# A transformer block on one core: the last part of the program in another order, from the same list scheduler with other constants

## Chip, core and metric

The kernel runs on one core of one Trainium2 chip. Its time is device time in microseconds (us) of one launch, from the first to the last instruction of the program with what the device adds around them. Less is better. The engines of a core work beside each other, each strictly through its own queue of instructions: PE (TensorE, matmuls), PEld (its weight loads), DVE (VectorE), ACT (ScalarE), POOL (GpSimd) and SP (SyncE, which here only issues transfers). An instruction waits at the head of its queue until what it needs is there, and everything behind it waits too.

## The reference

One block with adaptive layer norm: windowed causal attention with 32 heads of 16, and a gated feed-forward layer. Cut to what is computed (S = 2048 rows, D = 512, F = 1792, window W = 256, float32 throughout):

```python
mod = (silu(c) @ w_mod).reshape(1, 6, 1, -1)
sa, ca, ga, sb, cb, gb = (mod[:, i] for i in range(6))
h = layernorm(x) * (1 + ca) + sa
q, k, v = heads(h @ wqkv)                      # 32 heads of 16
p = softmax(where(0 <= i - j < W, q @ k.T * 16 ** -0.5, -1e9))
x = x + ga * (merge(p @ v) @ wo)
h = layernorm(x) * (1 + cb) + sb
x = x + gb * ((silu(h @ w1) * (h @ w3)) @ w2)
```

## The kernel before

Float32 precision is had from pairs: a matrix is split in a high part (a rounded copy, made by ACT) and a low part (the rest, made by DVE or POOL with a subtraction), and a product of two matrices is three matmuls, high by high, high by low and low by high (`PARTS`). Every operand that PE multiplies in the later stages thus needs one ACT and one DVE or POOL instruction ahead of it.

**Start and attention.** The rows are four blocks b = 0 to 3 of 512 rows, the heads eight groups g of four. Attention is 32 units u = (g, b). Each unit makes scores (L750, with a mask added by PE at L753, or by DVE at L758, or with two blocks merged by DVE at L768), probabilities on ACT (L762, L771), window masks on POOL (`affine_select`, L778 and L795) and values (L726), and stores its output `os` to `o_dr[b]` in HBM (L818). Ahead of its scores run the maxima of its rows: trial scores (L500), DVE maxima (L507), their transposition (L522, L527), and a small transfer of them into `ring` (L531). The order of all of this was written out by hand as due times (`X`, `Y`).

**The end, from a list schedule.** Whatever falls due after `TS` = 232 of those time units (the last three units), and all that follows attention, is ordered by the class `Sched`: each operation has an engine, an estimated duration, a key (a wish for when) and dependencies, and `deal()` goes through model time, always giving the engine its ready operation with the smallest key. The remaining attention operations are put in at fixed model times, `us(t)`, which `TW` stretches. Transfers are modelled by one wire of `RATE` GB/s. PSUM banks are handed out by use, at most `CAPS` of each use at once. Keys and the choice of engine come from the table `K`. The model sets nothing but the order: on the chip each engine follows its queue and waits where data are missing.

What it orders, in the program's words:

- `load_wo` (L1040, splits at L962 and L963): the output projection's weights `wo`.
- `o_sums` (L1061, L1065, L1066): softmax sums are read from `o_dr`, inverted by DVE (`RECIPROCAL`), and stored to `r_dr`; once for head groups 0 to 5 (tile `wqr`) and once for the last two (tile `mT`).
- `o_part(b, k)` for four slices k of each block: load of the attention output (L1083), load of the inverted sums spread over rows (L1078), their product (L1095), high part (ACT, L1087), low part (L1090). The tile is called `o` for b = 0, 2, 3 and `x1b` for b = 1; the loads land in `qkr`/`qk` (k = 0, 1) and `wq` (k = 2, 3).
- `o_proj(b)`: for each of the block's four row tiles, four groups of three matmuls (L1107), one group for each k; then `add_stats` adds x (L978, DVE), and gathers mean and squares (L983, L986 on ACT). x comes by L1046 into `x1a` and `x1b`.
- `ln_rstd` (L997 DVE, L1000 POOL, L1003 DVE) and `ln2`: the normalised rows (L1228 on ACT), their transposition (L1242 on PE), scale and shift (L1246 on ACT), differences (L1259) and splits (L1265 ACT, L1267 DVE or POOL) into the operands `b`.
- The feed-forward layer in two halves of the rows, each as seven pairs p of column tiles. A half uses a seven-product scheme in place of eight: `up` makes seven products of six matmuls each (L1371) with operands called B11, T2, T3, T1, B21, T4, B22; sums on DVE (L1399, L1403) and POOL (L1415); SiLU on ACT (L1394); splits of the result (L1443, L1446). `down` (L1465) multiplies by `w2` and L1470 adds to x. Weights come by `load_w` (L1165) and `load_w2` (L1209), split at L962 and L963. `half_rows`, `half_sums` and `load_b` prepare the second half's seven operands through HBM (L1346), again split at L962 and L963.

The table's entries that matter below: `by` (engines of L1095 and L1090 for each b and k), `su` (engine of the weights' low parts), `be` (engine of the low part of each second-half operand), and keys such as `pe`, `pl` (when `o_part` is wanted), `xb` (when x1a and x1b are), `w0` (the first weights).

## Time and profile before

| | us |
|---|---|
| median of 3 runs | 983.88 (979.4 to 986.37) |
| the profiled execution | 981.63 |
| its span, first to last instruction | 979.6 |
| PE busy in it | 942.7 (96%) |
| DVE, ACT, POOL busy | 746.8, 555.6, 503.9 |
| mean granted clock of PE | 0.990 |

Of the span, attention takes the stretch up to about 484 us, the output projection and the second layer norm that up to about 540 us, the first half of the feed-forward layer that up to about 740 us, and the second half the rest. A busy matmul at a halved granted clock counts as busy, so PE loses time in two ways: idle, and busy at a low clock. Both have to be read stretch by stretch. In the views below, a row of the timeline has the start, the time that the (merged) instructions took, engine, line, operation, tile written and tiles read, and in brackets the idle time of the engine ahead of it and what ended it. A row of the windows has the stretch, then busy time of PE, PEld, DVE, ACT and POOL (with the number of instructions), the granted clock of PE, the mean busy share of the 16 DMA engines, and GB/s.

### The profile page before, as it was taken

Reading aid. Unit: us, or ns where it says so; the run is one execution under the profiler, and the core shown is the slowest. Engines: PE = TensorE matmul, PEld = TensorE weight load, DVE = VectorE, ACT = ScalarE, POOL = GpSimd, SP = SyncE. Lnnn points to the kernel's source line nnn. Section 1 sums busy time; section 2 is a strip of 40 time slices with the busy share of each in tenths; the row PEclk is TensorE's granted clock in tenths of the full one; section 3 lists DMA queues with packets and bytes.
Section 4 is the critical chain, followed back from the end, with each engine's and each line's share of the span. In section 5 each row is a group of like instructions: output and inputs, shape, how many; then the busy total and the mean of one; then the engine's idle time right before and its main releaser. Section 6 shows DMA issues by size and latency. Waiting matters only on the chain.

```text
span 979.6 us, 17120 instructions
## 1 busy us (share of the span) xinstructions
PE 942.7 (96%) x5316; PEld 718.4 (73%) x5316; DVE 746.8 (76%) x2049; ACT 555.6 (57%) x1252; POOL 503.9 (51%) x725
## 2 busy tenths in 40 slices
PE   5999999999999999998889999999999999999998
PEld 3578777677767776775567888888887888888886
DVE  7776799898989899898566685866769765576545
ACT  3333787887878787876568945233445443423330
POOL 7441787777767786864464754654416122111320
PEclk9999999999999999999899999999999999999999
DMA  8521354444444444435893576756434432212102
GB/s 288 184 87 34 117 180 150 142 153 143 158 158 142 142 143 143 142 121 177 225 264 89 177 254 217 243 173 202 151 124 145 152 119 77 79 48 88 44 22 86
DMA packets 80670, 141.63 MB, mean 145 GB/s; under 512 B 9538, under 2 KB 22338, under 8 KB 80580
## 3 DMA queue, kind: packets, MB, share of 16 engines
q1 hardware_dynamic: 79860, 139.50, 44.0%
q10 hardware_dynamic: 720, 1.05, 0.4%
q8 instruction: 42, 0.69, 0.3%
q14 instruction: 48, 0.39, 0.1%
HBM read 85.72 MB, written 34.61 MB: 123 GB/s over the span
## 4 chain that ended last, share of the span: by engine, by line
PE 78%; DVE 7%; POOL 5%; DMA 4%; ACT 2%; issue 2%; SPq 1%; POOLq 0%; DVEq 0%; ACTq 0%
PE mx L1371 12%; PE st L1371 11%; PE mx L500 7%; PE st L1465 7%; PE pj L447 7%; PE st L750 7%; PE po L726 6%; PE mx L1465 6%; PE pj L1371 5%; PE st L664 3%; PE pj L1465 2%; POOL pt L778 2%; POOL qk L465 2%; PE mx L1107 1%; DMA w<-w2g 1%
## 5 line engine op out<-in xcount | busy, mean ns | idle before, releaser
L507 DVE CUSTOM_DVE_ANT_0 junk<-mx,mskq 128x384 bf16<-128x384 f32 (+2 forms) x512 | 256.4, 527 | 28.2 <-PE mx L500 26.7
L750 PE MATMUL st<-ring 100*128 100x384 f32 (+2 forms) x512 | 156.3, 347 | 5.1 <-ACT pt L771 3.3
L500 PE MATMUL mx<-ring 96*128 96x384 f32 (+2 forms) x512 | 155.1, 341 | 4.4 <-DVE st L768 1.5
L778 POOL TENSOR_SCALAR_AFFINE_SELECT pt<-pt 128x256 f32<-128x256 f32 x268 | 108.3, 407 | 68.9 <-ACT pt L771 58.5
L447 PE MATMUL pj<-hT,wq 128*128 128x512 f32 x384 | 136.5, 405 | 1.5 <-DVE hT L364 1.2
L500 PEld LDWEIGHTS mx<-ring 96*128 96x128 f32 x512 | 93.9, 190 | 37.5 <-DVE mt L507 24.6
L771 ACT ACTIVATE pt<-st 128x256 f32<-128x256 f32 x268 | 96.1, 386 | 44.0 <-DVE st L768 36.4
L1415 POOL TENSOR_TENSOR t<-t,t 128x512 f32<-128x512 f32 x28 | 40.3, 1439 | 155.6 <-DVE t L1403 153.4
L750 PEld LDWEIGHTS st<-ring 100*128 100x128 f32 x512 | 95.9, 191 | 27.1 <-issue 8.6
L726 PE MATMUL po<-pt,vS 128*17 128x384 f32 (+2 forms) x1408 | 97.3, 393 | 3.6 <-POOL pt L778 3.2
L465 POOL TENSOR_TENSOR qk<-qkr,qk 128x512 fp32r<-128x512 f32 x64 | 82.7, 1292 | 15.9 <-ACT qkr L453 15.6
L768 DVE COPY_PREDICATED st<-later,st 128x128 f32<-128x128 uint8 x268 | 72.3, 292 | 11.4 <-PE st L750 8.2
L447 PEld LDWEIGHTS pj<-hT,wq 128*128 128x128 f32 x384 | 71.9, 191 | 8.6 <-DVE hT L364 1.5
L963 POOL TENSOR_TENSOR w<-w,w 128x512 fp32r<-128x512 f32 (+2 forms) x31 | 42.4, 1385 | 63.2 <-ACT w L962 63.2
L726 PEld LDWEIGHTS po<-pt,vS 128*17 128x17 f32 x1408 | 33.1, 98 | 49.8 <-issue 20.9
L762 ACT ACTIVATE pt<-st 128x384 f32<-128x384 f32 (+2 forms) x128 | 52.8, 434 | 18.7 <-DVE st L758 12.6
L1371 PE MATMUL st<-b,w 128*128 128x512 f32 x246 | 61.6, 392 | 0.1
L876 POOL TENSOR_TENSOR e<-e 128x128 f32<-128x128 f32 x64 | 41.9, 659 | 31.0 <-DMA e<-in_w 27.8
L1394 ACT ACTIVATE g<-t 128x512 f32<-128x512 f32 x42 | 26.5, 630 | 55.2 <-POOL t L1415 40.3
L1371 PE MATMUL mx<-b,w 128*128 128x512 f32 x234 | 57.6, 390 | 0.0
L795 POOL TENSOR_SCALAR_AFFINE_SELECT sm<-sm 128x256 f32<-128x256 f32 x109 | 41.9, 407 | 27.8 <-ACT sm L785 24.0
L1403 DVE TENSOR_TENSOR t<-mx,t 128x512 f32<-128x512 f32 x49 | 33.6, 686 | 27.3 <-PE mx L1371 26.9
(270 smaller groups left out, 2080.6 us busy)
## 6 DMA issues: line engine op xcount, KB each, us to landing
ring<-qk SPq DMA_DIRECT2D x192, 128.0 KB
o_dr<-os SPq DMA_DIRECT2D x32, 256.0 KB
w<-wsum SPq DMA_DIRECT2D x14, 512.0 KB
w<-w2g SPq DMA_DIRECT2D x14, 512.0 KB
jb<-in_w SPq DMA_DIRECT2D x24, 256.0 KB
wraw<-in_w SPq DMA_DIRECT2D x7, 768.0 KB
w<-wraw SPq DMA_DIRECT2D x14, 384.0 KB
vS<-in_wmod SPq DMA_DIRECT2D x20, 256.0 KB
```

The source lines that it names most:

```text
L447: nc.tensor.matmul(v["ps"], WQ[g][w][:, n // 3], hTp(i, n // 3, b * BT, BT), start=(n == 0), stop=(n == 3 * KC - 1))
L465: nc.gpsimd.tensor_tensor(out=v[n], in0=v["raw"], in1=v[1].bitcast(F32), op=ALU.subtract)
L500: nc.tensor.matmul(v[i][:, :n], queries(NS, a, gq, 1), keys(NS, hh, a, k0, gq + 1 - k0), start=True, stop=True)
L507: nc.vector.tensor_tensor_reduce(out=junk[:, :n], in0=v[i][:, :n], in1=mskq[:, 3 * P - n:], scale=1.0, scalar=-3e38, op0=ALU.add, op1=ALU. ...
L726: nc.tensor.matmul(po[32 * i:32 * i + DH + 1, qb * P:(qb + nq) * P], vS[:, kb, 4 * g + i], pts[i // 2][:, i % 2, c0:c0 + nq], start=first, ...
L750: nc.tensor.matmul(ps[:, :nq], keys(NM, hh, a, kb, 1), queries(NM, a, kb, nq), start=True, stop=not plus)
L762: nc.scalar.activation(held[u, j, a][:, hh, :nq], v[j, a, hh][:, :nq], AF.Exp, scale=SCALE)
L768: nc.vector.copy_predicated(ps[:, 0], later, ps[:, 2])
L771: nc.scalar.activation(held[u, j, a][:, hh, :2], v[j, a, hh][:, :2], AF.Exp, scale=SCALE)
L778: nc.gpsimd.affine_select(out=pt[:, :, 2 * m], in_=pt[:, :, 0], **w)
L1371: nc.tensor.matmul(ps(bk), WT[s, n][w][:, col], BB[t, k][r], start=start and c == 0, stop=stop and c == 5, skip_group_check=True)
L1465: nc.tensor.matmul(ps(bk), tiles[hk + (h,)][:, i * P:(i + 1) * P], w2_of(last, y, f), start=(m == 0), stop=(m == 5))
```

## The change

No function is edited. Three constants of the scheduler and the table `K` are changed: `RATE` from 320 to 240 GB/s, `TW` from (235.0, 1.75, 1.45) to (243.0, 1.7, 1.5), so that the last units end later in the model, and `CAPS` from three transposition and four product banks to four and five. The instructions are the same ones but for merging, with other engines for some low parts and another order.

```diff
-CAPS = dict(tp=3, up=4, dn=5)
+CAPS = dict(tp=4, up=5, dn=5)
...
-RATE = 320.0
+RATE = 240.0
...
-TW = (235.0, 1.75, 1.45)
+TW = (243.0, 1.7, 1.5)
...
-K = dict(be=(('POOL', 'DVE'), ('DVE', 'POOL'), ('DVE', 'DVE'), ('DVE', 'POOL'), ('POOL', 'POOL'),
+K = dict(be=(('POOL', 'POOL'), ('POOL', 'DVE'), ('POOL', 'POOL'), ('DVE', 'POOL'), ('POOL',
...
```

**Place 1, the last attention unit.** PE, in unit 31: scores are L750 and L753, values L726, and L1107 is the output projection of block 0 (`wo` its weights, `o` its operand, high and low parts). One piece of the difference:

```order
 L753 MATMUL st<-mskr,identr 128x2x128
-L750 MATMUL st<-ring 128x384 x2
-L726 MATMUL po<-pt,vS 17x384 x4
-L726 MATMUL po<-pt,vS 17x256 x4
-L726 MATMUL po<-pt,vS 17x128 x4
+L1107 MATMUL pj<-wo_7622,o_7624 128x512
+L1107 MATMUL pj<-wo_7623,o_7624 128x512
+L1107 MATMUL pj<-wo_7622,o_7625 128x512
+L750 MATMUL st<-ring 128x384 x2
+L726 MATMUL po<-pt,vS 17x384 x4
+L726 MATMUL po<-pt,vS 17x256 x4
+L726 MATMUL po<-pt,vS 17x128 x4
```

Three groups of three such matmuls (k = 0, 1, 2 of the first row tile) now stand among the scores and values of unit 31, the first as shown and two more behind the values; before, all of them stood behind its last scores.

POOL at the same place, before (L778 masks probabilities `pt`; L963 is a low part of `wo`; L1095 and L1090 belong to `o_part`):

```order
L778 AFFINE_SELECT pt<-pt 128x2x128 x2
L963 TENSOR_TENSOR wo_7623<-wo_7623,wo_7622 128x512
L778 AFFINE_SELECT pt<-pt 128x2x128 x6
L1090 TENSOR_TENSOR o_7625<-qkr,o_7624 128x512
L1095 TENSOR_TENSOR qk_7961<-qk_7961,qk_7966 128x512
L778 AFFINE_SELECT pt<-pt 128x2x128 x2
L1095 TENSOR_TENSOR wq_7976<-wq_7976,wq_7979 128x512
L778 AFFINE_SELECT pt<-pt 128x2x128 x2
```

And now:

```order
L778 AFFINE_SELECT pt<-pt 128x2x128 x2
L963 TENSOR_TENSOR wo_7623<-wo_7623,wo_7622 128x512
L778 AFFINE_SELECT pt<-pt 128x2x128 x2
L1095 TENSOR_TENSOR qkr<-qkr,qk_7829 128x512
L778 AFFINE_SELECT pt<-pt 128x2x128 x4
L1090 TENSOR_TENSOR o_7625<-qkr,o_7624 128x512
L1095 TENSOR_TENSOR qk_7916<-qk_7916,qk_7942 128x512
L778 AFFINE_SELECT pt<-pt 128x2x128 x2
L1090 TENSOR_TENSOR o_7625<-qk_7916,o_7624 128x512
L778 AFFINE_SELECT pt<-pt 128x2x128 x4
```

The product of slice k = 0 has come from DVE to POOL and stands four masks earlier. On DVE the one that stood ahead of four merges (L768) is gone; the first L1095 there is now that of k = 2, behind three more merges. On SP, the loads of slice 0 (`qkr`, `qk_7829`) stand ahead of the transfer of unit 31's maxima (L531) instead of behind it; two of the four `RECIPROCAL`s that stood behind those maxima on DVE stand ahead of them; and four of the eight loads of `x1a`, which stood ahead of slice 0, stand behind slice 2.

**Place 2, the layer norm of block 0.** ACT, from the third row tile's squares (L986) on. L962 splits weights of the feed-forward layer (`w`), L1228 makes the normalised rows. Before:

```order
L986 ACTIVATE mx,sqB_8180<-x1a,nmB_8179 128x512
L1087 ACTIVATE o_7624<-qkr 128x512
L1087 ACTIVATE o_7624<-qk_8177 128x512
L962 ACTIVATE w_8224<-w_8225 128x1024
L986 ACTIVATE mx,sqB_8180<-x1a,nmB_8179 128x512
L962 ACTIVATE w_8226<-w_8227 128x768
L986 ACTIVATE st,sqB_8318<-x1a,nmB_8317 128x512
L962 ACTIVATE w_8226<-w_8227 128x1024
L1087 ACTIVATE o_7624<-wq_8233 128x512
L962 ACTIVATE w_8228<-w_8229 128x512 x2
L986 ACTIVATE st,sqB_8318<-x1a,nmB_8317 128x512
L1228 ACTIVATE wqr<-x1a,nbB_8182,rsB_8181 128x512
```

And now:

```order
L986 ACTIVATE mx,sqB_8173<-x1a,nmB_8172 128x512
L1087 ACTIVATE o_7624<-qkr 128x512
L986 ACTIVATE mx,sqB_8173<-x1a,nmB_8172 128x512
L962 ACTIVATE w_8217<-w_8218 128x768
L962 ACTIVATE w_8217<-w_8218 128x1024
L986 ACTIVATE st,sqB_8305<-x1a,nmB_8304 128x512
L1228 ACTIVATE wqr<-x1a,nbB_8175,rsB_8174 128x512
L1228 ACTIVATE e_8337<-x1a,nbB_8175,rsB_8174 128x512
L1087 ACTIVATE o_7624<-qk_8236 128x512
L986 ACTIVATE st,sqB_8305<-x1a,nmB_8304 128x512
L1228 ACTIVATE e_8354<-x1a,nbB_8175,rsB_8174 128x512
L1228 ACTIVATE e_8361<-x1a,nbB_8175,rsB_8174 128x512
```

The weight splits that stood ahead of the fourth L986 and of L1228 now stand behind them, but for two. On DVE, ten instructions stood between L997 and L1003 (the last step ahead of L1228), among them two L1090 and an L963; now there are four. PE's first transposition (L1242) stands behind the same number of L1107 matmuls less six, and block 2's products of slices 2 and 3, which PE needs next, get their L1090 on DVE behind an L963 of weights.

**Place 3, the start of the second half.** DVE, before; `b_8213` is the low part of T2 for k = 0, the second operand that PE needs:

```order
L1399 TENSOR_TENSOR g_10225<-t_10311,g_10225 128x512
L1399 TENSOR_TENSOR g_10262<-t_10300,g_10262 128x512
L1399 TENSOR_TENSOR g_10271<-t_10285,g_10271 128x512
L1470 TENSOR_TENSOR x1a<-mx,x1a 128x512
L1470 TENSOR_TENSOR x1a<-pj,x1a 128x512
L1470 TENSOR_TENSOR x1a<-mx,x1a 128x512
L1446 TENSOR_TENSOR qk_10410<-g_10271,qkr 128x512
L1446 TENSOR_TENSOR qk_10413<-g_10225,qk_10401 128x512
L963 TENSOR_TENSOR b_8213<-b_8213,b_8212 128x512
L963 TENSOR_TENSOR b_8217<-b_8217,b_8216 128x512
```

And now, with `b_8208` as T2 for k = 1 and `b_8202` as T1 for k = 0:

```order
L1470 TENSOR_TENSOR x1a<-mx,x1a 128x512
L963 TENSOR_TENSOR b_8208<-b_8208,b_8207 128x512
L1399 TENSOR_TENSOR g_10282<-t_10312,g_10282 128x512
L1399 TENSOR_TENSOR g_10246<-t_10301,g_10246 128x512
L1399 TENSOR_TENSOR g_10273<-t_10284,g_10273 128x512
L1470 TENSOR_TENSOR x1a<-st,x1a 128x512
L1470 TENSOR_TENSOR x1a<-mx,x1a 128x512
L1470 TENSOR_TENSOR x1a<-pj,x1a 128x512
L1470 TENSOR_TENSOR x1a<-st,x1a 128x512
L963 TENSOR_TENSOR b_8202<-b_8202,b_8201 128x512
```

T2 for k = 0 is now `b_8206`, third in a row of eleven low parts on POOL (there were nine, with T2 for k = 1 second); the order of the eleven is B11 twice, T2, T3 twice, T1, B21 twice, T4, B22 twice.

More of the change, by code (lines that the diff above doesn't have):

```diff
@@ L289 @@
       (("POOL", "DVE"),) * 3 + (("DVE", "DVE"),), (("POOL", "POOL"),) * 4)
-K = dict(be=(('POOL', 'DVE'), ('DVE', 'POOL'), ('DVE', 'DVE'), ('DVE', 'POOL'), ('POOL', 'POOL'),
-         ('POOL', 'POOL'), ('POOL', 'POOL')), hr=0.021, de=-0.648, wo=1.036, x1=5.767, xb=-9.184,
-         xl=-0.033, os=-0.126, ol=(-55.169, -1.421, -42.722, 0.185), pl=(41.373, 8.795, -1.822,
-         -41.728), pe=(7.549, 48.95, 1.65, 13.385), o=(-125.938, 2.261, 13.943, 7.688), n=(1, 1,
-         2, 2), w0=0.067, l2=0.718, f=2.007, fl=9.546, by=((('DVE', 'POOL'), ('POOL', 'DVE'),
-         ('POOL', 'DVE'), ('DVE', 'POOL')), (('DVE', 'POOL'), ('DVE', 'DVE'), ('DVE', 'DVE'),
-         ('DVE', 'POOL')), (('POOL', 'DVE'), ('POOL', 'POOL'), ('DVE', 'DVE'), ('DVE', 'DVE')),
-         (('POOL', 'POOL'), ('DVE', 'DVE'), ('DVE', 'DVE'), ('DVE', 'POOL'))), w=0.444, dn=2.464,
-         ds=-0.135, l3=-1.275, sw=('POOL', 'DVE', 'DVE', 'POOL'), su=(('POOL', 'POOL', 'DVE',
-         'POOL'), ('POOL', 'DVE', 'POOL', 'DVE'), ('DVE', 'DVE', 'DVE', 'DVE')), sr=(('POOL',
-         'DVE', 'DVE', 'DVE', 'DVE', 'DVE', 'DVE', 'DVE', 'DVE', 'DVE', 'POOL'), ('DVE', 'POOL',
-         'POOL', 'POOL', 'POOL', 'POOL', 'DVE', 'DVE', 'DVE', 'DVE', 'POOL')))
+K = dict(be=(('POOL', 'POOL'), ('POOL', 'DVE'), ('POOL', 'POOL'), ('DVE', 'POOL'), ('POOL',
+         'POOL'), ('POOL', 'DVE'), ('POOL', 'POOL')), hr=1.228, de=-0.011, wo=0.363, x1=5.427,
+         xb=-11.259, xl=0.182, os=0.09, ol=(-29.26, -4.358, -61.448, -4.772), pl=(23.674, -19.281,
+         -2.126, -37.597), pe=(1.308, 32.004, -0.229, 9.552), o=(-92.491, -1.503, 76.848, -7.065),
+         n=(1, 1, 2, 2), w0=0.298, l2=0.646, f=3.115, fl=5.405, by=((('POOL', 'POOL'), ('POOL',
+         'POOL'), ('DVE', 'DVE'), ('POOL', 'POOL')), (('POOL', 'POOL'), ('POOL', 'DVE'), ('DVE',
+         'DVE'), ('POOL', 'POOL')), (('POOL', 'DVE'), ('DVE', 'DVE'), ('DVE', 'DVE'), ('DVE',
+         'DVE')), (('POOL', 'POOL'), ('DVE', 'DVE'), ('DVE', 'DVE'), ('DVE', 'POOL'))), w=0.25,
+         dn=1.72, ds=0.103, l3=-4.114, sw=('POOL', 'DVE', 'DVE', 'POOL'), su=(('POOL', 'DVE',
+         'DVE', 'POOL'), ('POOL', 'POOL', 'POOL', 'DVE'), ('DVE', 'DVE', 'DVE', 'POOL')),
+         sr=(('POOL', 'DVE', 'DVE', 'DVE', 'POOL', 'DVE', 'DVE', 'DVE', 'DVE', 'DVE', 'DVE'),
+         ('POOL', 'DVE', 'POOL', 'DVE', 'POOL', 'DVE', 'DVE', 'POOL', 'DVE', 'POOL', 'POOL')))
 @with_exitstack
```

## The prediction

> **What bounds the kernel now.** I read the page's slices first, then busy time and clock by stretches, then PE's timeline where it idles, then the queues that PE waited for. In the slices each digit is a fortieth of the span:
>
> ```profile
> PE   5999999999999999998889999999999999999998
> ...
> PEclk9999999999999999999899999999999999999999
> ```
>
> PE is full almost everywhere. Its holes stand in slices 19 to 22, about 440 to 540 us, where the granted clock falls too, and there is one small hole near 740 us. The stretches say how large:
>
> ```profile
> 440.00:484.00 44.00, 35.60 (x248) 21.16 (x247) 29.00 (x95) 26.49 (x69) 20.37 (x37) 0.88 0.66 194
> 484.00:508.00 24.00, 24.00 (x124) 19.04 (x124) 16.69 (x33) 13.16 (x27) 15.78 (x10) 1.00 0.96 255
> 508.00:526.00 18.00, 14.99 (x55) 11.32 (x54) 11.70 (x24) 13.17 (x24) 8.81 (x7) 0.81 0.76 212
> 526.00:540.00 14.00, 12.17 (x65) 9.72 (x64) 9.76 (x18) 13.46 (x25) 5.17 (x4) 1.00 0.01 2
> 540.00:740.00 200.00, 200.00 (x884) 163.14 (x883) 143.00 (x194) 101.28 (x158) 104.25 (x110) 1.00 0.59 199
> 740.00:760.00 20.00, 18.35 (x79) 14.48 (x78) 19.91 (x23) 8.16 (x14) 11.82 (x8) 1.00 0.25 89
> 760.00:976.00 216.00, 215.89 (x932) 174.69 (x930) 135.22 (x195) 73.78 (x117) 39.45 (x29) 1.00 0.24 77
> ```
>
> From 540 to 740 and from 760 to 976 PE idles 0.1 us in 416: no order can win there, it can only lose. The rest can be counted. Idle: 44.00 - 35.60 = 8.4 us in 440 to 484, 3.0 in 508 to 526, 1.8 in 526 to 540, 1.65 in 740 to 760, together 14.9. Lost to the clock: 35.60 x 0.12 = 4.3 and 14.99 x 0.19 = 2.8, together 7.1. So 22 us is all that a new order of these instructions could win, the last attention units' own chains included.
>
> PE's rows at the holes, and one that shows the speed:
>
> ```profile
> 456.82 0.44 PE L750 MATMUL st<-ring 100*128 100x384 f32 x1 [2.10 <-ACT pt L771]
> ...
> 474.10 0.41 PE L726 MATMUL po<-pt,vS 128*17 128x128 f32 x8 [2.38 <-POOL pt L778]
> ...
> 483.94 2.29 PE L1107 MATMUL pj<-wo,o 128*128 128x512 f32 x9
> ...
> 511.12 0.33 PE L1242 MATMUL mx<-ident,wqr 128*128 128x128 f32 x1 [2.02 <-ACT wqr L1228]
> ```
>
> Nine products of L1107 take 2.29 us at full clock, about 0.23 each and the last one's tail. The short windows show when the clock falls:
>
> ```profile
> 470.70:474.10 3.40, 1.02 (x17) 0.24 (x9) 1.10 (x3) 1.18 (x3) 0.87 (x3) 1.00 1.00 270
> 474.10:477.50 3.40, 2.94 (x15) 1.93 (x15) 0.88 (x3) 2.24 (x6) 3.33 (x5) 0.58 1.07 267
> 477.50:481.00 3.50, 3.39 (x26) 1.34 (x26) 0.61 (x2) 1.32 (x4) 2.31 (x3) 0.50 1.06 304
> ...
> 508.30:511.70 3.40, 1.13 (x5) 0.47 (x3) 3.37 (x8) 3.19 (x7) 0.82 (x1) 1.00 1.01 257
> 511.70:515.10 3.40, 2.67 (x7) 1.90 (x8) 0.88 (x4) 3.40 (x9) 2.42 (x2) 0.57 1.03 277
> 515.10:518.50 3.40, 3.40 (x9) 2.63 (x9) 3.10 (x5) 1.31 (x3) 2.69 (x4) 0.50 0.99 268
> ...
> 528.70:532.20 3.50, 2.43 (x13) 1.73 (x12) 3.47 (x5) 3.47 (x7) 1.46 (x1) 1.00 0.00 0
> 532.20:535.60 3.40, 2.69 (x14) 2.06 (x12) 2.47 (x6) 3.09 (x8) 0.00 (x0) 1.00 0.01 2
> ```
>
> After a window with PE busy for 1.02 or 1.13 of 3.4 us, the next two are granted 0.50 to 0.58; after one with 2.43 busy, the next has 1.00. A hole of two microseconds thus costs more than itself, where little else fills the window.
>
> The Trainium skill ("TensorE: Matmul & The Clock Gate", Part 1) has the clock fall to half only after a whole idle window of about 3.4 us. No hole here is that long and the clock fell, so here the trace differs and decides; by the rule the holes would not cause the slow stretches, the clock term of about 4 us below would drop out, and the sum would be about -3.4.
>
> **Place 1, the last attention unit.** Why PE waited 2.38 us at 474.10 is read backwards: values waited for POOL's mask, that for ACT, that for a merge on DVE, and DVE stood in L1095, behind the load of inverted sums:
>
> ```profile
> 468.56 1.05 POOL L778 TENSOR_SCALAR_AFFINE_SELECT pt<-pt 128x256 f32<-128x256 f32 x2 [1.88 <-ACT pt L771]
> 473.16 0.88 POOL L778 TENSOR_SCALAR_AFFINE_SELECT pt<-pt 128x256 f32<-128x256 f32 x2 [3.55 <-ACT pt L771]
> ...
> 475.24 1.28 POOL L1095 TENSOR_TENSOR qk<-qk,qk 128x512 f32<-128x512 f32 x1
> ```
>
> ```profile
> 455.22 0.94 DVE L1065 RECIPROCAL mT<-mT 32x128 f32<-32x128 f32 x1 [1.00 <-DMA wqr<-o_dr]
> ...
> 471.78 0.69 DVE L1095 TENSOR_TENSOR qkr<-qkr,qk 128x512 f32<-128x512 f32 x1 [1.71 <-DMA qk<-r_dr]
> 472.39 0.49 DVE L768 COPY_PREDICATED st<-later,st 128x128 f32<-128x128 uint8 x2
> ```
>
> ```profile
> 468.27 3.39 DMA qk<-r_dr
> ```
>
> ```profile
> 467.03 0.71 SPq L1061 DMA_DIRECT2D mT<-o_dr  x1
> ...
> 491.92 0.34 SPq L818 DMA_DIRECT2D o_dr<-os  x1
> ```
>
> The load was issued at 468.27 and took 3.39 us; DVE idled 1.71 for it with two merges queued behind. In the new order this L1095 (slice 0) is on POOL, four masks earlier, and its two loads stand ahead of unit 31's maxima on SP, so that they land long before; the DVE wait of 1.71 goes. What is late next: POOL now does slice 1 (L1095) ahead of the mask that the values need. Its load keeps its place on SP, behind the same load of sums (467.03 + 0.71), so it lands at about 467.8 + 3.4 = 471.2; with 1.28 for L1095 and 0.88 for two masks PE gets its mask at about 473.4 against 474.04 before. So only about 0.6 of the 2.38 is won by the masks, and the first group of L1107, which stands ahead of two scores, waits for POOL's L1090 of slice 0 until about 470.9 (it stands behind the masks that ended at 469.6, and takes some 1.28), and the second for slice 1's until about 475, some 0.9 us behind the values. On DVE two more RECIPROCALs (0.94 each) stand ahead of unit 31's maxima; against them one has left unit 30's, and the wait of 1.00 at 455.22 goes, so I cost them at nothing, from -1 to +1. In all PE is some 1.7 us later at its last values, and saves 9 x 0.23 = 2.1 behind them: about even. The gain is in the clock: with products and values, the window from 470.7 holds about 2.3 us of PE work, not 1.02, near the 2.43 that kept the clock. The two windows behind it lost 2.94 x 0.42 + 3.39 x 0.50 = 2.9 us, of which I take 2.5, since a wait stays in the first of them. Place 1: **-2.5**, from -8.8 (the holes of 2.1 and 2.4 and the 4.3 of clock all gone) to +2.4 (new waits of 0.9 and 1.5, and no clock won).
>
> The transfers behind it are a matter of sums, not of places. From 465 to 521 us the queue is full:
>
> ```profile
> DMA packets 7950, 13.92 MB, mean 249 GB/s; under 512 B 871, under 2 KB 1783, under 8 KB 7947
> ```
>
> With the stretch's 255 GB/s at a share of 0.96, full means some 266 GB/s, so 256 KB take 1.0 us, and the four loads of x1a moved behind slice 2 make everything behind them 4 us later: slice 3 of block 0 is the eighth load behind slice 1's, lands at about 471.2 + 8 = 479.2 and is ready, with two POOL instructions of 1.28 and ACT's between, by about 482.5, and PE wants it behind the last scores at about 484. Block 1's four slices and a store, nine transfers, land by about 488, and PE wants the first at about 495. I cost this at nothing; what hides it is 1.5 us of attention for slice 3, and 5 us for block 1.
>
> The Trainium skill ("DMA: Bandwidth & Descriptors", Bandwidth) lists 341 GB/s for 1 MB issued from GpSimd on one core, nearer the old constant than the new one. This trace has 249 over the stretch with the engines full, and decides; at 341 the waits for loads would not be there and the whole change would be worth about nothing.
>
> **Place 2, the layer norm of block 0.** The three holes at 511 to 513 and the slow clock behind them follow from one chain of L986, L997, L1000, L1003, L1228:
>
> ```profile
> 500.97 0.67 ACT L986 ACTIVATE mx<-x1a,nmB 128x512 f32<-128x512 f32 x1
> ...
> 510.27 0.80 ACT L1228 ACTIVATE wqr<-x1a,nbB,rsB 128x512 f32<-128x512 f32 x1
> ```
>
> ```profile
> 503.64 1.02 POOL L1000 TENSOR_TENSOR rsB<-sqB,nhalf 128x4 f32<-128x4 f32 x1
> ```
>
> ```profile
> 507.20 2.48 DVE L1090 TENSOR_TENSOR o<-wq,o 128x512 fp32r<-128x512 f32 x1
> 509.60 0.15 DVE L1003 TENSOR_TENSOR nbB<-nmB,rsB 128x4 f32<-128x4 f32 x1
> ```
>
> The fourth L986 ran at 500.97, behind splits of weights just loaded. POOL was done at 504.66; L1003 came at 509.60, behind three DVE instructions of which one L1090 took 2.48; L1228 at 510.27. PE came to L1242 at 511.12 - 2.02 = 509.1. In the new order PE comes there without the six L1107 (1.4 us), at about 507.6 - 1.7 = 505.9. The chain: the last unit's output is stored at about 490.3 (491.92 less 1.7), block 2's slice 0, next on SP, lands at about 493.5, multiplied on POOL to 495.3, its ACT part to 496, the fourth L986 to 497, L997 and L1000 (1.02) to 498.3, L1003 behind one RECIPROCAL (0.95) at 499.7, the four L1228 (0.80 each, with an L1087 and an L986 of 0.7 between) done at about 504.5. So 1.4 us of slack, and the hole goes. What is late next: block 2's slices 2 and 3. Their L1090 on DVE stand behind an L963 whose ACT part stands behind the last L1228, so they end at about 509 and 509.7, while PE, after L1242 and two groups, wants slice 2 at 507.8: a wait of 1.3. The window then has some 2.1 us of work, between 1.13 (falls) and 2.43 (holds); I take half of the 2.8. Place 2: -3.0 - 2.8 + 1.3 + 1.4 = **-3.1**, from -5.8 to 0.
>
> From 526 to 540 PE idles 1.8 us for ACT's and DVE's operands of block 0 and 1; the same instructions feed it in both orders, all starting earlier by what was won: nothing, plus or minus 1.
>
> **Place 3, the start of the second half.**
>
> ```profile
> 750.71 1.20 PE L1371 MATMUL mx<-b,wo 128*128 128x512 f32 x4 [1.65 <-DVE b L963]
> ```
>
> ```profile
> 739.43 4.86 DVE L1399 TENSOR_TENSOR g<-t,g 128x512 f32<-128x512 f32 x3
> ...
> 748.91 3.55 DVE L963 TENSOR_TENSOR b<-b,b 128x512 fp32r<-128x512 f32 x4
> ```
>
> ```profile
> 736.10 10.63 POOL L963 TENSOR_TENSOR b<-b,b 128x512 fp32r<-128x512 f32 x7
> ```
>
> PE waited 1.65 us for T2's low part, on DVE at 748.91 behind three L1399 that took 4.86 us beside POOL's row (1.62 each). Now T2 for k = 0 is third on POOL, ready at about 736.1 + 3 x 1.52 = 740.7 (seven in 10.63 are 1.52 each), and that for k = 1 is on DVE ahead of the L1399. The last of eleven ends at about 736.1 + 11 x 1.52 = 752.8; PE, which alternates with L1465 here, wants B22 at about 760, T1 (POOL's sixth, 745.2, and DVE's at about 747) at 752.6. So **-1.65**, from -1.65 to 0.
>
> What stands elsewhere (weights' splits on other engines, transfers of the first half) is hidden by PE at 100%: 0, up to +1.5 should one cover fail.
>
> **Sum.** -2.5 - 3.1 - 1.65 = -7.25 against the execution's 981.63 (span 979.6 and 2.03 around it): 974.4. That execution is 2.25 below the median of the runs, 983.88; against the median the forecast is **976.6**.
>
> **Rivals.** (1) *All holes close* (0.15): place 1 wins its 8.8, place 2 its 5.8, place 3 1.65, together 16.2: 967.6, and the case spans 967 to 972. For it: nothing in the new queues stands ahead of a mask but slices 0 and 1. Against it: 2.1 us of the hole at 456.82 belong to DVE's maxima, of which none is removed.
>
> (2) *The holes move* (0.18): L1107 among the scores costs what the clock gives, block 2's slices cost what L1003 gave, and only place 3 and a microsecond or two stay: about -2.5, so 981.4. For it: both new waits are found above, only their sizes are guessed.
>
> (3) *Slower: slice 1 holds POOL's masks* (0.12). The pair `qk_7916`, `qk_7942` decides. Each microsecond that it lands after 471.2 goes into the wait for masks, values and scores behind it, one for one, and a window under about 1.3 us of PE work costs 2.9 of clock again. Places 2 and 3 win 4.75; with place 1 even and its clock not won, the point is a lateness of about 4.75 us. SP could make it, by standing at the store of sums, which waits for a RECIPROCAL. At 8 us: 983.88 + 8 - 4.75 = 987.1.
>
> (4) *The slow clock is not due to the holes* (0.05) and stays where it is: 0 at place 1, -3.0 + 1.3 = -1.7 at place 2, -1.65 at place 3, together -3.35: 980.5. The windows quoted speak against it. By the clock-gate page of the Trainium skill it would come out so.
>
> (5) *The queue is faster than counted* (0.02), the waits for loads are chance of one execution, and nothing is won: 983.9. The full share at 249 GB/s speaks against it. This is what the DMA page of the Trainium skill would give.
>
> **How the numbers follow.** The forecast (972 to 981) has 0.48. One per cent, about what a measurement of this kernel can tell from no change, is 9.8 us: below 974.0 lie rival 1 and a fifth of the forecast, 0.25; above 993.7 a lateness of some 14 us in rival 3, 0.04; the rest, 0.71, is the same within 1%. The range takes in most of rival 1 and rivals 2, 4 and 5, and of rival 3 what lies below 986: 968.5 to 986.
>
> **What would show it.** Place 1 right: no DVE wait for `qk<-r_dr` among L768, nine L1107 `pj` among unit 31's scores, granted clock near 1 in the windows after them; wrong: POOL idle for a load at L1095 ahead of L778, for over 2 us. Place 2 right: L1228 done before PE's first L1242, and a wait of about 1.3 us on L1107 of block 2; wrong: L986 or L1228 behind L962 that waits for a transfer. Place 3 right: PE full from 740 to 760; wrong: a wait for `b`. The forecast falls if PE, after 540, waits where it did not: that would be the weights' splits on POOL, which no row of before can show.

## The result, and the profile after

The changed kernel takes 973.48 us, the median of four runs (972.31 to 974.12), beside 984.23 for the kernel before with the runs of the same chip (979.40 to 986.37): a ratio of 0.9905, with a 95% interval of 0.9882 to 0.9929 (the two medians alone give 0.9891). The same kernel once more, in another set of runs, gave 972.47 beside 981.47: 0.9902 (0.9883 to 0.9920). So the gain is one per cent, small but clear of the scatter. Ratios go by the undisturbed runs: one run of e9a_l1003 below took 1145.87 us at a granted clock of 0.75 and is left out of its ratio. The profiled execution took 973.01, its span 971.3.

The slices of the changed kernel's page:

```profile
PE   5999999999999999998898999999999999999998
...
PEclk9999999999999999999799999999999999999999
```

The hole near 740 us is gone; about 440 to 540 us PE still waits. Its stretches (columns as before the change):

```profile
440.00:484.00 44.00, 37.08 (x251) 21.46 (x249) 26.85 (x90) 25.55 (x66) 21.98 (x37) 0.88 0.65 203
484.00:508.00 24.00, 24.00 (x128) 19.12 (x127) 16.36 (x37) 17.44 (x37) 11.73 (x9) 1.00 0.87 228
508.00:526.00 18.00, 15.26 (x74) 12.54 (x74) 14.68 (x19) 15.92 (x27) 11.64 (x8) 0.91 0.83 226
526.00:540.00 14.00, 14.00 (x65) 11.58 (x64) 13.56 (x34) 11.65 (x26) 9.72 (x8) 1.00 0.11 31
...
740.00:760.00 20.00, 20.00 (x87) 15.90 (x86) 17.68 (x21) 11.35 (x20) 16.38 (x11) 1.00 0.22 72
```

Idle time is 6.9 us in the first (it was 8.4), 2.7 in the third (3.0), none in the fourth (1.8), none in the last (1.65). But the kernels run ahead of each other, so equal times are not equal work. Three instructions of PE's queue serve as marks: unit 26's first values (L726), well ahead of the first change, the last values of attention, and the first L1304, behind the first layer norm. Before the change, from PE's timeline:

```profile
414.49 1.49 PE L726 MATMUL po<-pt,vS 128*17 128x128 f32 x24
...
489.69 1.49 PE L726 MATMUL po<-pt,vS 128*17 128x384 f32 x24
...
553.29 0.27 PE L1304 MATMUL mx<-ident,wqr 128*128 128x128 f32 x1
```

and after it:

```profile
413.43 1.49 PE L726 MATMUL po<-pt,vS 128*17 128x128 f32 x24
...
488.33 1.49 PE L726 MATMUL po<-pt,vS 128*17 128x384 f32 x24
...
545.55 0.27 PE L1304 MATMUL mx<-ident,wqr 128*128 128x128 f32 x1
```

The first mark is 1.06 us earlier although nothing ahead of it was changed: that is chance of one execution. Between the marks lie 75.20 and 63.60 us before, 74.90 and 57.22 after, and to the end of the span 426.31 and 425.75. By this pair of profiles place 1 won 0.3 us, the stretch with place 2 won 6.4, and the rest 0.6. L1304 itself stands some 1.1 us further forward in PE's new order. Without the wait of 1.65 the last part would have been 424.66 before, and PE's busy time there says the same: 420.95 us behind the mark before, in 1833 instructions, and 422.01 after, in 1839. So the layer norm's share is about 5.3 and place 3's about 1.65.

The experiments left these orders alone in one part or another, so the same distances can be read in eight profiles:

| order | first to second mark, place 1 | second mark to L1304 | L1304 to the end |
|---|---|---|---|
| before: three profiles (before, e9a, e9b) | 75.2, 77.3, 76.6 | 63.6 (before alone) | 426.3, 426.3, 426.3 |
| after: five (after, after_again, e1, e2, e11) | 74.9, 73.2, 72.8, 75.8, 73.6 | 57.2, 58.6, 57.7, 58.4 (without e2) | 425.8, 425.8, 425.6, 425.7 (without e11) |
| mean won | 2.3 | 5.6, of which 1.1 by L1304's place | some 0.55, and these 1.1 |

So one pair of profiles is misleading by 2 us at place 1. On the means, place 1 won 2.3, the layer norm 4.5 and place 3 1.65: 8.45 in all. With three profiles of one order and five of the other, and a spread of 2 to 3 us at place 1, its 2.3 is an estimate.

**Place 1 after.** PE in units 30 and 31; the first three waits are new:

```profile
455.69 0.92 PE L500 MATMUL mx<-ring 96*128 96x384 f32 x2 [0.95 <-DVE mt L507]
...
459.11 0.41 PE L726 MATMUL po<-pt,vS 128*17 128x128 f32 x8 [1.30 <-POOL pt L778]
...
461.94 0.40 PE L522 MATMUL mx<-ident,mr 128*32 128x128 f32 x1 [1.88 <-DVE mr L516]
...
470.81 1.20 PE L1107 MATMUL pj<-wo,o 128*128 128x512 f32 x3
...
473.95 0.41 PE L726 MATMUL po<-pt,vS 128*17 128x128 f32 x8 [0.38 <-POOL pt L778]
```

The 2.38 us for a mask are down to 0.38, and the nine products of L1107 stand among the scores with 0.17 us of wait in all. In their place PE now waits for DVE's maxima, behind four `RECIPROCAL`s, and for a mask behind POOL's split of `wo`. The last of the four, and POOL's split:

```profile
458.09 0.95 DVE L1065 RECIPROCAL wqr<-wqr 96x128 f32<-96x128 f32 x1 [0.72 <-DMA wqr<-o_dr]
```

```profile
456.93 1.28 POOL L963 TENSOR_TENSOR wo<-wo,wo 128x512 fp32r<-128x512 f32 x1 [4.11 <-ACT wo L962]
458.16 0.89 POOL L778 TENSOR_SCALAR_AFFINE_SELECT pt<-pt 128x256 f32<-128x256 f32 x2
```

**The layer norm after.** L1003 on DVE, the first L1228 on ACT and PE's first L1242, from three timelines:

```profile
500.38 0.57 DVE L1003 TENSOR_TENSOR nbB<-nmB,rsB 128x4 f32<-128x4 f32 x1
```

```profile
500.99 0.82 ACT L1228 ACTIVATE wqr<-x1a,nbB,rsB 128x512 f32<-128x512 f32 x1 [0.78 <-DVE nbB L1003]
```

```profile
506.22 0.27 PE L1242 MATMUL mx<-ident,wqr 128*128 128x128 f32 x1
506.33 0.49 PE L1242 MATMUL mx<-ident,e 128*128 128x128 f32 x3
506.57 3.00 PE L1107 MATMUL mx<-wo,o 128*128 128x512 f32 x12
```

L1228 comes 9.3 us earlier than before, and PE neither waits at L1242 nor at block 2's products behind it. The next hole is a new one, for a bank that ACT's L1246 has to clear, behind five L1265:

```profile
523.12 2.93 PE L1107 MATMUL st<-wo,o 128*128 128x512 f32 x6 [2.74 <-ACT t L1246]
```

```profile
519.69 2.71 ACT L1265 ACTIVATE b<-t 128x512 fp32r<-128x512 f32 x5
522.30 0.76 ACT L1246 ACTIVATE t<-st,modc 128x512 f32<-128x512 f32 x1
```

**Where the clock falls.** In windows laid on the steps of the granted clock itself, 3.41 us each (PE busy is the second number, the clock the third from the end):

```profile
457.81:461.23 3.42, 0.96 (x10) 0.43 (x10) 3.07 (x9) 1.75 (x4) 1.81 (x4) 1.00 0.68 194
461.23:464.64 3.41, 2.70 (x16) 2.09 (x20) 1.95 (x5) 2.27 (x7) 2.20 (x4) 0.50 0.01 2
464.64:468.05 3.41, 3.41 (x27) 1.59 (x20) 0.00 (x0) 0.95 (x2) 1.25 (x3) 0.50 0.51 174
474.88:478.29 3.41, 2.51 (x10) 1.54 (x10) 1.34 (x4) 1.71 (x6) 0.92 (x3) 1.00 1.06 284
478.29:481.71 3.42, 3.42 (x25) 1.79 (x28) 0.66 (x2) 1.36 (x4) 2.78 (x4) 0.50 0.94 310
```

The half clock comes in whole windows, each time behind a window in which PE was not full: 0.96 us busy the first time, 2.51 the second. At a mean of 0.88, place 1 still loses 12% of its 37.08 us to the clock, as before. But that is one pair of profiles. In the order of the table, the half clock takes 3, 5 and 4 windows between the first two marks in the old order, and 3, 3, 2, 3 and 2 in the new one: 1.4 fewer on the mean, at up to 1.7 us each. With so few profiles this is a hint, and not shown.

### The profile page after: what moved, and what is told of

Read it like the earlier page. It is cut to its first block, busy times and chain, and to the rows that moved or that the text cites. A ratio compares the mean times of both kernels' runs of the same rounds, so it can differ in the third digit from the quotient of the medians.

```text
span 971.3 us, 17147 instructions
## 1 busy us (share of the span) xinstructions
PE 940.5 (97%) x5316; PEld 716.7 (74%) x5316; DVE 743.1 (77%) x2032; ACT 556.4 (57%) x1252; POOL 542.8 (56%) x742
## 4 chain that ended last, share of the span: by engine, by line
PE 83%; POOL 5%; DVE 5%; DMA 2%; issue 2%; ACT 1%; SPq 1%; POOLq 0%; DVEq 0%; ACTq 0%
PE st L1371 13%; PE mx L1371 11%; PE mx L500 7%; PE pj L447 7%; PE mx L1465 7%; PE st L750 7%; PE st L1465 7%; PE po L726 6%; PE pj L1371 5%; PE st L664 3%; PE pj L1465 2%; PE mx L1107 2%; POOL pt L778 2%; PE st L1107 2%; POOL qk L465 1%
## 5 line engine op out<-in xcount | busy, mean ns | idle before, releaser
L750 PE MATMUL st<-ring 100*128 100x384 f32 (+2 forms) x512 | 155.7, 346 | 2.1 <-ACT pt L771 1.2
L778 POOL TENSOR_SCALAR_AFFINE_SELECT pt<-pt 128x256 f32<-128x256 f32 x268 | 109.3, 410 | 62.8 <-ACT pt L771 52.4
L750 PEld LDWEIGHTS st<-ring 100*128 100x128 f32 x512 | 96.0, 191 | 23.0 <-issue 8.3
L726 PE MATMUL po<-pt,vS 128*17 128x384 f32 (+2 forms) x1408 | 97.7, 394 | 3.2 <-POOL pt L778 2.9
L963 POOL TENSOR_TENSOR w<-w,w 128x512 fp32r<-128x512 f32 (+2 forms) x36 | 59.8, 1678 | 62.1 <-ACT w L962 44.6
L768 DVE COPY_PREDICATED st<-later,st 128x128 f32<-128x128 uint8 x268 | 72.2, 291 | 17.1 <-PE st L750 13.7
L726 PEld LDWEIGHTS po<-pt,vS 128*17 128x17 f32 x1408 | 33.1, 98 | 49.5 <-issue 22.0
L1371 PE MATMUL st<-b,w 128*128 128x512 f32 x258 | 64.1, 390 | 0.0
L1403 DVE TENSOR_TENSOR t<-st,t 128x512 f32<-128x512 f32 x52 | 35.7, 687 | 36.4 <-PE st L1371 31.2
L1443 ACT ACTIVATE wq<-g 128x512 fp32r<-128x512 f32 x28 | 17.7, 634 | 67.9 <-PE st L1465 40.6
L1371 PEld LDWEIGHTS st<-b,w 128*128 128x128 f32 x258 | 48.4, 188 | 10.2
```

What stands on the lines that cost most here:

```text
L726: nc.tensor.matmul(po[32 * i:32 * i + DH + 1, qb * P:(qb + nq) * P], vS[:, kb, 4 * g + i], pts[i // 2][:, i % 2, c0:c0 + nq], start=first, ...
L750: nc.tensor.matmul(ps[:, :nq], keys(NM, hh, a, kb, 1), queries(NM, a, kb, nq), start=True, stop=not plus)
L768: nc.vector.copy_predicated(ps[:, 0], later, ps[:, 2])
L778: nc.gpsimd.affine_select(out=pt[:, :, 2 * m], in_=pt[:, :, 0], **w)
L963: sch.op(eng, lambda: on_eng(eng).tensor_tensor(out=lo(), in0=src(), in1=hi().bitcast(F32), op=ALU.subtract), tt(eng, n), key, kl + kh, kl ...
L1371: nc.tensor.matmul(ps(bk), WT[s, n][w][:, col], BB[t, k][r], start=start and c == 0, stop=stop and c == 5, skip_group_check=True)
```

## The experiments

All ratios are to the kernel before on the same chip in the same set of runs. In several kernels single operations are moved in the scheduler's finished list: `item(tag, n)` is the n-th operation of a part of the program, `move` puts it before or behind another one. The tag `('ln2', 0)` has the first layer norm (0: L997, 1: L1000, 2: L1003, 3 to 6: L1228), `('os', b)` the inverses of block b (1 and 4: `RECIPROCAL`, 2 and 5: their stores), `'w'` the first weights, and `('op', b, k)` a slice.

**Place 3 alone, `be` old (e1_be).**

```diff
-be=(('POOL', 'POOL'), ('POOL', 'DVE'), ('POOL', 'POOL'), ('DVE', 'POOL'),
-    ('POOL', 'POOL'), ('POOL', 'DVE'), ('POOL', 'POOL'))
+be=(('POOL', 'DVE'), ('DVE', 'POOL'), ('DVE', 'DVE'), ('DVE', 'POOL'),
+    ('POOL', 'POOL'), ('POOL', 'POOL'), ('POOL', 'POOL'))
```

> The changed kernel with the old entry `be` alone (engines of the second half's low parts), so that T2's low part stands behind three L1399 on DVE again. Theory, step 3 of the prediction: PE waits for a low part `b` in 735 to 760 us again, about 1.65 us, and the time is that much over the changed kernel's 973.0 to 973.5: about 975. Rival: the wait went because all that stands ahead now comes earlier or on other engines, and `be` has no part in it: no wait there, and 973 to 973.5.

0.9927 (0.9905 to 0.9950), 976.18 us; but PE has no wait at 740, and L1304 lies 425.6 us ahead of the end, as in the changed kernel. The median lies above what either case named. The rival holds for `be` alone: its interval overlaps that of the changed kernel, and nothing at place 3 separates the two profiles. DVE's timeline shows why there is no wait:

```profile
732.59 2.23 DVE L963 TENSOR_TENSOR b<-b,b 128x512 fp32r<-128x512 f32 x2
734.74 0.68 DVE L1399 TENSOR_TENSOR g<-t,g 128x512 f32<-128x512 f32 x1
```

T2's low part is on DVE again, but ahead of the L1399: the key of these operations, `l3`, had gone from -1.275 to -4.114. So both entries were put back:

```diff
-l3=-4.114
+l3=-1.275
```

> The changed kernel with two old entries, `be` and `l3` (the key of the second half's operands). With both, one low part of T2 stands on DVE behind the three L1399 again; with `be` alone (e1_be) the key had put both ahead of them. Theory: either entry is enough to bring T2's low part forward, and with both old PE waits 1 to 2 us for `b` at 735 to 760: 974.5 to 975.5. Rival: the wait went because all of the first half ends in another order, and neither entry has a part in it: no wait, 973 to 974.

0.9950 (0.9930 to 0.9971), 977.26 beside 972.47. From L1304 to the end 427.74 us, 2.0 more than in the changed kernel. The wait is back, in another dress: PE waits for a bank that L1470 has to clear, and L1470 stands on DVE behind three low parts.

```profile
739.12 5.17 DVE L963 TENSOR_TENSOR b<-b,b 128x512 fp32r<-128x512 f32 x3
744.22 0.68 DVE L1470 TENSOR_TENSOR x1a<-mx,x1a 128x512 f32<-128x512 f32 x1
```

```profile
744.95 0.73 PE L1465 MATMUL mx<-w,qkr 128*128 128x512 f32 x2 [1.78 <-DVE x1a L1470]
```

In the new order the new key alone is enough to win place 3 (e1), and with both entries old it is lost; whether the new `be` alone would be enough, no run shows. Of the 4.8 us between the medians the profile accounts for 2.0.

**The layer norm late again (e2_late).**

```diff
+move(item(('ln2', 0), 2), behind=item('w', 8))
+for n in (6, 5, 4, 3):
+    move(item(('ln2', 0), n), behind=item(('ln2', 0), 2))
```

> The changed kernel with block 0's layer norm late again, nothing else: L1003 stands behind the split L963 of the third weights on DVE (some 6.5 us later, at about 507), and the four L1228 on ACT behind it. Theory, step 2: PE stands at L1242 from 506.2 until the four L1228 are done at about 510, a hole of 3 to 4 us as in the kernel before, and the clock halves behind it for one or two windows (1.5 to 3 us): 977 to 980. Rival: from 515 to 531 ACT and DVE set the pace, so what PE loses at 506 it no longer loses at 523, where it now waits 2.7 us: within 1.5 of 973.5.

0.9959 (0.9943 to 0.9975), 978.20 us. The theory holds:

```profile
510.72 0.47 PE L1242 MATMUL mx<-ident,wqr 128*128 128x128 f32 x1 [2.82 <-ACT wqr L1228]
```

With the 0.23 at each of the next three rows that is 3.5 us of hole, and two windows of half clock follow. The wait for L1246 stays at 2.73, so nothing is given back there. From the last values to L1304 it is 65.64 us, 7.6 more than the mean, in a profile that was the slowest of this kernel's ten runs (982.95); by the ratios, 0.9959 against 0.9905, the loss is some 5 us.

**The same edit the other way, in the kernel before.** First L1003 alone on DVE (e9a_l1003), then also L1228 ahead of the last three splits on ACT (e9b_rows):

```diff
+move(item(('ln2', 0), 1), behind=item(('ln2', 0), 0))
+move(item(('ln2', 0), 2), before=item(('op', 2, 0), 4))
...
+for n in (3, 4, 5, 6):
+    move(item(('ln2', 0), n), before=item('w', 10))
```

> The kernel before with one instruction moved: L1003 of block 0 stands right behind the first L978 after L997 on DVE, so that it runs at about 504.8 in place of 509.6. Step 2 of the prediction named two reasons for the late L1228, DVE's queue and ACT's splits. If DVE's was enough, L1228 comes at about 505 to 507 and 3 to 6 us are won: 977 to 980. If ACT's splits bind too (two waits for loads, 0.32 and 1.34 us, stand ahead of L1228 there, and L1228 followed its predecessor on ACT without a gap at 510.27), nothing is won: within 1.5 of the kernel before.

> The kernel before with L1003 moved as in the run beside it, and the four L1228 ahead of the last four splits of weights on ACT as well. Theory, step 2: PE has no wait at L1242 (3.0 us with its three rows) and no half clock behind it (3.1 us): 5 to 6 us faster than the kernel before, 977 to 979. Rival: the splits are now late, or block 2's slices: a new wait behind 513 us takes half of it back: 2 to 3 us faster, 980 to 982.

e9a: 1.0025 (1.0015 to 1.0036), a little slower. An earlier DVE is not enough: L1003 was done at 507.0, and L1228 came 8 us later, behind a split on ACT that waited for its load. (In the kernel before the two queues lay close: L1003 was done at 509.75, and ACT came to L1228 at 510.27.)

```profile
506.88 0.16 DVE L1003 TENSOR_TENSOR nbB<-nmB,rsB 128x4 f32<-128x4 f32 x1 [0.35 <-POOL rsB L1000]
```

```profile
513.41 1.15 ACT L962 ACTIVATE w<-w 128x512 fp32r<-128x512 f32 x2 [3.39 <-DMA w<-w2g]
...
515.17 0.80 ACT L1228 ACTIVATE wqr<-x1a,nbB,rsB 128x512 f32<-128x512 f32 x1
```

e9b: 0.9996 (0.9980 to 1.0012), nothing won, less even than its rival; its 981.75 us lies in the rival's range only because the kernel before took 981.73 in this set. L1242 no longer waits; block 2's products do, 0.57 and 1.73 us, with the half clock behind them:

```profile
514.85 5.57 PE L1107 MATMUL mx<-wo,o 128*128 128x512 f32 x16 [1.73 <-DVE o L1090]
```

This is the wait that the prediction had put behind L1242 in the changed kernel. There it is absent. In the old order, where PE takes slice 2 right behind L1242, it is there.

**Table and constants apart (e5_table, e6_const).** The edit of e5_table is shown; e6_const makes the opposite one in the kernel before.

```diff
-CAPS = dict(tp=4, up=5, dn=5)
-RATE = 240.0
-TW = (243.0, 1.7, 1.5)
+CAPS = dict(tp=3, up=4, dn=5)
+RATE = 320.0
+TW = (235.0, 1.75, 1.45)
```

> The new table `K` with the three old constants (`RATE` 320, `TW` and `CAPS` as before). Block 0's L1228 then stand behind two splits of weights, as in the changed kernel, and the second half's operands are loaded by the new key `l3`. Theory: the table carries the gain at places 2 and 3, the constants only fit it: PE has no wait at L1242 and none at 740 to 760, and the time is 972 to 976. Rival: the constants carry it, since with 320 GB/s the scheduler puts splits and products ahead of data that are not there: waits for slices and weights come back, 979 to 984.

> The three new constants with the old table `K`. Here L1003 has come to the front on DVE, but the four L1228 stand behind four splits of weights on ACT (three ahead of them in the kernel before wait for loads). Theory: the splits wait for their loads and L1228 with them, so a hole at L1242 of 1 to 3 us stays, as does the wait of 1.65 us for `b` at 740 to 760: 977 to 982. Rival: the constants alone carry the gain: no hole at L1242, 972 to 976.

e5: 1.0041 (1.0027 to 1.0056); e6: 1.0048 (1.0030 to 1.0065). Both are slower than the kernel before, by less than half a per cent, and both (985.99 and 986.42 us) lie above both of their cases. What e5's theory said of the waits holds: PE waits no more than 0.38 us at the first L1242 rows, and not at all from 740 to 760. Neither kernel has the wait for `b` at 740, e6 in spite of its old `be` and `l3`, but both have others, up to 5.82 us; two of the largest of e5, then of e6:

```profile
497.31 5.28 PE L1107 MATMUL st<-wo,x1b 128*128 128x512 f32 x22 [2.39 <-DVE x1b L1090]
...
551.89 0.47 PE L1304 MATMUL st<-ident,t 128*128 128x128 f32 x1 [2.75 <-ACT t L1295]
```

```profile
515.18 0.48 PE L1242 MATMUL st<-ident,g 128*128 128x128 f32 x1 [2.14 <-ACT g L1228]
...
537.03 5.34 PE L1371 MATMUL st<-b,w 128*128 128x512 f32 x12 [5.82 <-ACT t L1406]
```

Neither half alone brings the gain. That the keys fit only the constants beside which they stand is a reading of these two runs; which key or constant makes the new waits was not tried.

**The nine products out of attention (e3_proj).**

```diff
+for n in (0, 1, 2):
+    move(item(('oproj', 0), n), before=item(('oproj', 0), 3))
```

> The changed kernel with the three groups of products (nine L1107, 2.1 us) taken out of unit 31 and put back behind its last scores, PE's order alone. Step 1 of the prediction said even: values 1 to 2 us earlier, and the 2.1 us back behind 484 us; the granted clock is halved in one or two windows of 474 to 482 as it is now: within 1 us of 973.5. Rival A: the products only fill time in which PE waits for masks: without them 2.1 us more, and a window more at half clock (1.7): 975.5 to 977.5. Rival B: they hold the values back one for one, and without them it is 1 to 2 us faster: 971.5 to 972.5.

0.9925 (0.9902 to 0.9948), 975.67. Rival A: the distance to the last values is 74.14, no shorter than the changed kernel's mean of 74.1, and that from there to L1304 is 60.82, longer by 2.8. So the products seem to fill time that PE waits anyway; it is one profile, against a spread of 3 us at place 1.

**Place 1's new waits (e4_sums, e10_wo, e12_all).** Three steps on each other: the inverses behind unit 31's maxima; block 1's x behind slice 3's loads and no longer ahead of `wo`; the last splits of `wo` behind the first probabilities, block 1's inverse behind one more merge, and one L1246 ahead of two L1265. The edit is that of e12_all; in the other two, block 1's inverse and its store stand at `item('wo', 8)` and `item(('op', 0, 2), 1)`.

```diff
+for b, n, to in ((0, 4, item('wo', 5)), (1, 1, item(('os', 1), 4)), (0, 5, item(('op', 0, 1), 0)), (1, 2, item(('os', 1), 5)),
+                 (2, 2, item(('op', 1, 2), 0)), (3, 2, item(('op', 1, 2), 0))):
+    move(item(('os', b), n), before=to)
+for b in (3, 2):
+    move(item(('os', b), 1), behind=item(('op', 0, 2), 4))
+move(item('wo', 1), before=item('wo', 4))
...
+for n in (7, 6, 5, 4):
+    move(item('x1', n), behind=item(('op', 0, 3), 1))
...
+for n in (7, 10):
+    move(item('wo', n), before=item(('op', 0, 0), 3))
+move(item('wo', 11), behind=item('wo', 10))
+move(item(('ln2', 0), 41), before=item(('ln2', 0), 31))
```

> The changed kernel with the four RECIPROCAL that stand ahead of unit 31's last maxima (L1065, four times 0.94 us on DVE) put behind them, with their stores, and the first split of `wo` one place later on ACT and POOL. Theory: the holes of 0.95, 1.30 and 1.88 us at 455 to 462 are due to these, and the half clock from 461.2 to 468.1 (3.1 us) to the holes: 4 to 7 us faster, 966.5 to 969.5. Rival: from 465 to 521 us the transfer queue is full, so PE comes earlier to slices and weights that do not: a new wait between 475 and 510, and less than 2 us won, 971.5 to 973.5. Rival: the clock falls in other windows instead: 2 to 4 us won, 969.5 to 971.5.

> The kernel of e4_sums with one thing more: the four loads of block 1's x (1 MB on the transfer queue) stand behind slice 3's loads, and no longer ahead of those of `wo`. In e4_sums ACT stood 2.66 us in all at its four splits of `wo` for their loads, and PE 2.90 us at L750 for what stood behind them. Theory: with the loads earlier that wait goes, and the half clock behind it: 3 to 6 us faster than the changed kernel beside it, 967.5 to 970.5. Rival: POOL's products or the inverses on DVE are late next, as each fix here has brought up another wait: less than 1.5 us faster, 972 to 974.

> The kernel of e10_wo with three moves more: the last two splits of `wo` (ACT) stand behind unit 31's first probabilities, with POOL's L963 behind them; block 1's inverse (DVE) stands behind one more merge; and at 519 to 523 ACT's first L1246 of the second k stands ahead of two L1265. Theory: each wait had one cause left. The hole of 2.67 us at L750, behind ACT's waits of 1.10 and 0.92 us for `wo`, shrinks below 0.8; the 1.05 behind DVE's inverse goes; the 2.75 at L1107 behind L1246 falls to about 1.7, two L1265 of 0.54 us less. Together 3 to 4 us, and up to 3 us of half clock: 967 to 970.5. Rival: the waits come up at other instructions once more, or the half clock stays for the hole at 521: less than 1.5 us under the changed kernel's 972.5 to 973.5.

e4: 0.9916 (0.9896 to 0.9936), 974.35 us; e10: 0.9925 (0.9904 to 0.9946), 973.40; e12: 0.9904 (0.9887 to 0.9920), 973.29. None is faster than the changed kernel, and the times of e10 and e12 are those of their rivals. In e4 the waits for DVE and the mask shrink, and PE waits 2.90 us instead for what stands on ACT behind four splits, each of which waits for its load:

```profile
456.93 0.63 ACT L962 ACTIVATE wo<-wo 128x512 fp32r<-128x512 f32 x1 [0.70 <-DMA wo<-wog]
457.95 0.63 ACT L962 ACTIVATE wo<-wo 128x512 fp32r<-128x512 f32 x1 [0.39 <-DMA wo<-wog]
...
459.79 0.63 ACT L962 ACTIVATE wo<-wo 128x512 fp32r<-128x512 f32 x1 [0.94 <-DMA wo<-wog]
461.04 0.63 ACT L962 ACTIVATE wo<-wo 128x512 fp32r<-128x512 f32 x1 [0.63 <-DMA wo<-wog]
```

In e10 two of them still wait (1.10 and 0.92), and PE 2.67. In e12 that is gone: the distance to the last values is 69.25 us, 4.8 less than the mean, and no window from 436 to 555 us has less than the full clock. (That is this execution: its mean clock is 0.996, that of the other three 0.989 to 0.993.) But 2.7 come back between there and L1304 (60.66), where one wait became three:

```profile
521.61 1.67 PE L1107 MATMUL st<-wo,o 128*128 128x512 f32 x6 [1.71 <-ACT t L1246]
523.84 0.33 PE L1242 MATMUL pj<-ident,wqr 128*128 128x128 f32 x1 [0.56 <-ACT t L1246]
...
526.00 1.65 PE L1107 MATMUL mx<-wo,o 128*128 128x512 f32 x6 [1.50 <-ACT t L1246]
```

What is left of 2.1 us by the marks lies in this profile under an attention that began 3 us later, and in the medians it is not seen.

**The changed kernel once more (after_again).**

> The changed kernel unchanged, once more, beside the next two. Theory on the clock: the windows in which the half clock is granted lie on a grid that does not start with the program, so the same holes stand at the same instructions (2.74 at L1107 behind L1246, 1.9 at L522, 1.3 at L726), but the windows at half clock are other ones, one more or one less at a place, 1.5 us each: a single run within 4 us of the others. Rival: the half clock follows the holes alone and falls in the same windows as in the first profile, 460.5 to 467 and 477.5 to 481 and 522 to 525.

970.0 to 975.0 in six runs. The same holes stand at the same instructions, of 1.35 us at L522 and 0.38 at L726 this time, and 2.74 at L1107. The half clock came in three windows from 456.87 to 467.11 and one from 521.7, and in none at 478. The rows ahead of that one, which lost the clock in the first profile, keep it here, with the window's edge lying 0.6 us earlier against them (0.94 instead of 0.32 us ahead of the product that waits 0.17 for L1090, at 474.88 here and 475.20 there):

```profile
473.94:477.35 3.41, 2.60 (x15) 1.55 (x10) 1.10 (x3) 1.54 (x4) 0.99 (x2) 1.00 1.05 294
477.35:480.76 3.41, 3.33 (x31) 1.57 (x32) 0.90 (x2) 1.98 (x5) 2.85 (x5) 1.00 1.05 326
```

## Why the prediction was right, and where not

- *The total.* Forecast 976.6, measured 973.5, inside the range; the profiled execution fell by 8.6 us where the sum said 7.25. The marks explain 8.45 on the means. The medians fell by 10.75 in the first set and 9.0 in the second: the forecast had added 2.25 for the profiled execution's distance from its median, and after the change that distance is 0.5. The 2.25 was mostly chance of three runs: in four later sets of 7 to 27 runs the kernel before has medians of 981.47 to 982.84, near the profile's 981.63.
- *Place 1, -2.5.* 2.3 on the means, right in size, with luck in it, since the terms were not right one by one. The values are not 1.7 us late for the nine products: e3 found no cost of them, and the 2.38 of hole went down to 0.38. The term of the clock, -2.5, did not come in the first pair, with a mean clock of 0.88 on both sides; over the eight profiles some of it may have, by the windows counted above. Its reason failed: the bound of 2.43 us of work, above which a window keeps the clock, came from one window, laid half a microsecond off the clock's steps (on them it has 2.22). A window with 2.51 lost the clock, and one with 2.60, on nearly the same rows, kept it. The cost of the inverses, "at nothing, from -1 to +1", was too low: with the splits of `wo` they make the new waits of 0.95 to 1.88, which shrink or go when they are moved (e4). The DVE wait for slice 0's sums went as described.
- *The transfers, at nothing.* Right: in the changed kernel's timeline one product of blocks 0 and 1 waits for a slice, by 0.17 us (475.20, for POOL's L1090). From 465 to 521 us the queue is as full as before:

```profile
DMA packets 7824, 13.88 MB, mean 248 GB/s; under 512 B 849, under 2 KB 1649, under 8 KB 7821
```

- *Place 2, -3.1.* Under-sized: 4.5 with the stretch to 540 us. The chain was right (e2 puts the hole and the slow clock back). The new wait of 1.3 on block 2's slices and the 1.4 of half clock behind it did not come; e9b has them, with the old places of the slices. The L1090 of slices 2 and 3 ran when it was said, from 508.2 to 509.5, but PE does five groups of slices 0 and 1 first, the fifteen products from 506.57 to 510.09, where the prediction counted two groups. Of DVE's and ACT's queue, which the prediction named together, DVE's alone is not worth anything (e9a): ACT's splits, waiting for loads, hold L1228 as well. From 526 to 540 the 1.8 us went, and a wait of 2.74 with a window of half clock came at 523: the term "0, plus or minus 1" was short of a wait that the order of L1265 and L1246 on ACT would have shown.
- *Place 3, -1.65.* Right in size and in engine. The step named only the engines of `be`; e1 shows that the key `l3` does it without them. Nor does PE wait anywhere from 540 to 740, as the forecast had feared for the weights' splits on POOL: it idles 0.03 us there.
- *The rivals.* Case 1 (967.6) is not what happened; in e12 one execution had the full clock and still took 973.9. Case 2 (981.4) has the mechanism right, since holes did move, to 455 to 462 and to 523, but they took back less than was won. Cases 3, 4 and 5 are out: slice 1 did not hold the masks (0.38 us), the holes at 511 took their half clock with them and brought it back in e2, and 9 to 11 us were won. For case 4 the Trainium skill ("TensorE: Matmul & The Clock Gate", Part 1) says that the windows run freely, 3413 ns each, which the windows here bear out, and that the clock falls behind an idle window, which they do not: 0.96 and 1.13 us of work were not enough to hold it.

## What to carry to other kernels

Before an order is costed, each engine's queue has to be read for instructions that wait for a transfer, because whatever stands behind them waits too; that made many of the holes here, though the new one at 523 us is five splits long and waits for no load. Each hole closed in e4, e10 and e12 brought up another one, so a gain is to be measured between marks on the bound engine and not at the hole, and in several profiles. And a table of keys should be tried with its constants: here either half alone was slower than the old pair.
